# Loading the last v of an attention and spectral-mixing kernel on another queue, in two parts

## Chip, cores and metric

The kernel runs on one core of one Trainium2 chip. The metric is device time in microseconds (us) of one execution; lower is better. Inputs lie in the chip's memory (HBM) when the clock starts, and the output has to be there when it stops.

## What is computed

Two steps follow each other. The first is linear attention over 8 batches x 8 heads with 576 tokens of 64 features; the second mixes the tokens of each batch in the frequency domain, with one complex 512x512 matrix for each of 64 modes, and adds a gated product.

```python
def phi(x):
    proj = np.einsum('bhsd,df->bhsf', x, w_phi)                 # 64 -> 128 features
    proj = proj - np.max(np.abs(proj), axis=-1, keepdims=True)
    return np.concatenate([np.exp(proj), np.exp(-proj)], axis=-1)
q_p, k_p = phi(q), phi(k)
kv  = np.einsum('bhsf,bhsd->bhfd', k_p, v)
num = np.einsum('bhsf,bhfd->bhsd', q_p, kv)
den = np.einsum('bhsf,bhf->bhs', q_p, k_p.sum(2))[..., None] + 1e-06
x   = (num / den) as [8, 576, 512]

X = np.fft.rfft(x, axis=1)                                       # 64 modes are mixed
Yr = Xr @ w_r[m] - Xi @ w_i[m];  Yi = Xr @ w_i[m] + Xi @ w_r[m]
u = x + np.fft.irfft(Y, n=576, axis=1)
out = u + np.maximum(u @ w_ch, 0)
```

The matrices `w_r` and `w_i` are 64 x 512 x 512 in float32 each, and all of them have to be read once. They are the bulk of the 163.64 MB that the kernel reads.

## The kernel before

**Units.** Attention is cut into 16 units: 4 groups `g` of two heads by 4 pairs `bp` of batches. Each unit loads k and q (as bfloat16, converted on the way) and v (`vn`, float32, 128 partitions x 2 batches x 576 elements, 576 KB). Partition p of the load holds nine tokens in a row of one head. In memory that is one run of 2304 bytes for each of the two batches.

**Order.** A hand-written loop over `n` staggers the units: in one turn, unit n+1 has its rows of k and q projected, unit n is finished and unit n-1 goes into the frequency domain. `InOrder` keeps every engine's instructions in the order in which the program writes them. So an engine that waits holds up all that stands behind it.

**v in that loop.** `weigh_v` gets the weights of unit n, `ee`, on ScalarE. `weigh_v2` first copies `ee` into a column of `va` and then multiplies v by it in two VectorE instructions (`va<-vn,ee`), whose result TensorE needs in `kv`. Right after unit n's `weigh_v2`, the loop issues the load of v of unit n+2. The tile `vn` has two buffers, so this load takes the buffer that has just been read. Units 0 and 1 get their v on SyncE's queue (SP) at the start; units 2 to 15 get it on GpSimd's queue (POOL).

**Weights.** The mixing matrices come in 64 loads of 128 partitions x 4 modes x 2 rows x 512 (`wload`), read as float32 and written as bfloat16, in the order of the list `wq`. They are issued on POOL by `next_w`, between the loads of q, k and v, into nine rotating buffers `wt` and a few tiles that are not yet in use. `mix` uses one load: eight matmuls of 512 columns. Mixes are interleaved with attention (`some`), and when attention is over a second loop does the last 20 of them:

```python
    while mixq:
        key = mixq.pop(0)
        ...
        mix(*key, wts.pop(key), XTb[g % 2], bank)
        next_w(1)
        ...
            fill(n)
```

`fill` does the work that lies beside these mixes: products of the channels with `w_ch`, the tables of the inverse transform, and the sums that use finished modes. Its first call comes after the first `mix` of that loop. The finished modes are moved between partitions by small transfers on SP (`yall<-yst`, `zall<-zst`). The last stage sums the rest and stores the output on SP.

**Queues.** Loads with a change of type go through POOL; in the profile its DMA queue is q0 (software_dynamic). SP's is q1 (hardware_dynamic). Between the two loads at the start and the first `yall` store SP issues nothing. q8 carries TensorE's instructions.

**Line numbers.** Since `InOrder` issues each instruction, the profile gives line 37 (L37) for almost all of them. Instructions are told apart by tile: `vn`, `va`, `wt`, `XT` (the modes of x), `xs` (attention's output), `yall` and `zall`.

Of the kernel before, what the change touches and what calls it, by code (L numbers as in the profile page):

```python
# [10 lines left out]
F32 = mybir.dt.float32  # L11
# [6 lines left out]
B_, H_, S_, D_ = 8, 8, 576, 64  # L18
# [25 lines left out]
def kernel(  # L44
# [15 lines left out]
    pool, sp = InOrder(tc, nc.gpsimd), InOrder(tc, nc.sync)  # L60
# [25 lines left out]
    pin = pin_cm.__enter__()  # L86
# [7 lines left out]
    def load(t, src, g, bp, eng):  # L94
        eng.dma_start(
            t.rearrange("p b c d -> p b (c d)"),
            src[2 * bp:2 * bp + 2, 2 * g:2 * g + 2].rearrange("b h (p c) d -> (h p) b (c d)", c=9),
        )


    class Unit:
# [11 lines left out]
        def load_v(self, eng=pool):  # L113
            self.vn = pin.tile([128, 2, 9, D_], F32, name="vn")
            load(self.vn, v, self.g, self.bp, eng)

        def turn(self, src, dst, flat, part):

            rows = src.rearrange("p i c d -> p (i c d)")
            lo, hi = ((0, 4), (4, 9))[part]  # L120
            ptr = one([128, hi - lo, 128], BF16)
            for j in range(lo, hi):
                if flat or j < 4:
                    pe.transpose(ptr[:, j - lo, :], rows[:, j * 128:(j + 1) * 128], ident_b)
                elif j < 8:
                    n = 9 + 2 * (j - 4)
                    pe.transpose(ptr[:, j - lo, :], rows[:, n * 64:n * 64 + 128], ident_b)
                else:
                    for i in range(2):
                        pe.transpose(ptr[64 * i:64 * i + 64, j - lo, :], src[:, i, 8, :], ident_b)  # L130
            act.copy(dst[:, lo:hi, :], ptr)
# [227 lines left out]
    def next_w(n):  # L359
        for _ in range(n):  # L360
            if wq:
                key = wq.pop(0)
                wts[key] = wload(*key)
# [3 lines left out]
    units = [Unit(g, bp) for g in range(NG) for bp in range(NP)]  # L367
# [73 lines left out]
    def forward_table():  # L441

        for p0, p1, d, n in ((0, 128, 0, 4), (0, 64, 4, 1), (64, 128, 5, 1)):
            src = csf[p0:p1, min(d, 4):min(d, 4) + n]
            dst = CF[p0:p1, d:d + n]
            for x in range(2):
                dve.tensor_scalar_mul(
                    out=dst[:, :, :, x, :], scalar1=1.0 - 2.0 * x,
                    in0=src[:, :, x, :].rearrange("p c (t m) -> p c t m", t=2))
        dve.tensor_scalar(out=mi[:, 0:1], in0=pi, scalar1=0, scalar2=1,  # L450
                          op0=ALU.logical_shift_right, op1=ALU.bitwise_and)
        dve.tensor_copy(mf[:, 0:1], mi[:, 0:1])
        for i in range(2):
            for n in range(4):
                sign, b = ((-1.0, 1.0), (1.0, 0.0))[n % 2]
                dve.tensor_scalar(out=side[:, i, n:n + 1], in0=mf[:, 0:1],
                                  scalar1=sign * (1.0 - 2.0 * i), scalar2=b * (1.0 - 2.0 * i),
                                  op0=ALU.mult, op1=ALU.add)
# [29 lines left out]
    def some(n):  # L488
        for _ in range(n):
            if mixq:  # L490
                key = mixq.pop(0)
                mix(*key, wts.pop(key), XTb[key[0] % 2], lambda: one([128, DMODEL]))
                if key not in held:
                    next_w(1)
# [5 lines left out]
    def unit(i):  # L500
        return units[i] if 0 <= i < len(units) else None

    for n in range(-2, len(units) + 1):
        P, Q, K, R = (unit(n + i) for i in (-1, 0, 1, 2))
        X = 0 if n < 4 else 6 if n == 4 else 3
        if Q:
            Q.exp_q(0)
        if K:
            K.rows_k(0)
            K.exp_k(0)  # L510
        if Q:
            Q.weigh_v2()
            if unit(n + 2):
                unit(n + 2).load_v()
        if P:
            P.freq()
            assert not any(key[0] == P.g - 2 for key in mixq)
            P.keep_x()
            if P.bp == NP - 1:
                mixq += [key for key in order if key[0] == P.g and (P.g < 2 or key[1] < 12)]  # L520
        if Q:
            Q.cols_q(1)
            Q.exp_q(1)
        some(1 if X else 0)
        if K:
            K.rows_k(1)
            K.exp_k(1)
        if Q:
            Q.kv()
        some(2 if n == 4 else 0)  # L530
        if K:
            K.rows_q(0)
            K.rows_k(2)
            K.rows_q(2)
            K.rows_q(1)
        if Q:
            Q.cols_q(2)
            Q.keep_kv()
            Q.exp_q(2)
        if K:  # L540
            K.exp_k(2)
            K.weigh_v()
        some(1 if X else 0)
        if R:
            R.turn_k(0)
        if K:
            K.shift_q()
        if R:
            R.turn_k(1)
        if Q:  # L550
            Q.num(0)
        if K:
            K.cols_q(0)
        if R and unit(n + 4):
            unit(n + 4).load_k()
        if Q:
            Q.num(6)
        if R:
            R.turn_q(0)
            R.turn_q(1)  # L560
            if unit(n + 4):
                unit(n + 4).load_q()
        if Q:
            Q.num(12)
        some(X - 2 + (n == 12))
        if n == -1:
            forward_table()
        if n < 3:
            next_w((2, 3, 2, 3, 2)[n + 2])
        elif n == 3:  # L570
            next_w(1)
        if n == 6:
            pool.dma_start(wchb, moe_w_ch.rearrange("(dc p) e -> p dc e", p=128))
# [349 lines left out]
    while mixq:  # L923
# [13 lines left out]
        if left > 8:  # L937
            n = -(-max(len(todo) - A - 2, 0) // (left - 8))
        elif left == 8:
            n = 2  # L940
        else:
            n = math.ceil(len(todo) / max(left - 0.6, 0.4)) if left else 0
# [111 lines left out]
```

## Time and profile before

| | |
|---|---|
| three timed runs | 440.22, 440.20, 439.05 us (median 440.2) |
| profiled execution, first to last instruction | 438.5 us |
| its time apart from the span | not listed; the median of the timed runs is 1.7 us above the span, the lowest 0.55 us |
| TensorE (matmuls) busy | 332.0 us, 76% |
| VectorE busy | 296.4 us, 68% |
| ScalarE busy | 279.4 us, 64% |
| GpSimd busy | 113.0 us, 26% |
| read from HBM | 163.64 MB, 395 GB/s over the span with the writes |
| mean granted TensorE clock | 0.906 |

How to read what follows. Times on the left of a row are microseconds from the first instruction. A row of the timeline gives start, duration, engine, operation, what it writes and reads, how many were merged, and in brackets the idle time of that engine before it with what ended it. A row of the waits gives total, number of times and longest. A DMA has landed when its completion has been counted sixteen times, once for each of the 16 DMA engines that work for a core; the trace holds these sixteen steps with their times. The chain is followed back from the last instruction, at each step to what released it.

### The profile page before, as it was taken

The page shows a single profiled execution, that of the slowest core. Times are in us where ns is not written, and L with a number is a line of the kernel's source. Part 1 is how long each engine was busy: PE and PEld are TensorE (multiplying, and loading weights), DVE is VectorE, ACT ScalarE, POOL GpSimd, SP SyncE. Part 2 cuts the span into 40 slices and gives each one's busy share as a digit, 9 for nine tenths or more (in the row PEclk, how much of TensorE's full clock was granted, in tenths as well). Part 3 has the DMA queues.
Part 4 walks back from the last instruction along what each step waited for, and adds up shares of the span by engine and source line. Part 5 has one row for each costly group of instructions (what it writes and reads, how often), then busy time and mean ns, then how long its engine had stood idle before and what let it go on. Part 6 is the DMA issues. An engine that isn't in the chain of part 4 may idle for free.

```text
span 438.5 us, 10107 instructions
## 1 busy us (share of the span) xinstructions
PE 332.0 (76%) x4190; PEld 202.1 (46%) x4233; DVE 296.4 (68%) x583; ACT 279.4 (64%) x478; POOL 113.0 (26%) x151
## 2 busy tenths in 40 slices
PE   2687678688687687687787787284789999998993
PEld 1355456465465465455465555152444554333320
DVE  5667776765786877976986888243784333886684
ACT  3786786776986886875875876210553442665781
POOL 6232132113221222221222221121101111483072
PEclk9998796789998999996996998876899999999996
DMA  9999999999999999999999999999999999996787
GB/s 213 209 212 210 237 212 237 237 212 248 228 211 239 225 228 232 237 215 235 232 217 239 210 239 211 238 213 212 212 215 223 219 222 224 212 219 135 242 361 309
DMA packets 51710, 99.55 MB, mean 227 GB/s; under 512 B 2512, under 2 KB 13648, under 8 KB 51664
## 3 DMA queue, kind: packets, MB, share of 16 engines
q0 software_dynamic: 45232, 85.86, 99.7%
q1 hardware_dynamic: 6272, 12.98, 8.5%
q8 instruction: 33, 0.54, 0.5%
q14 instruction: 13, 0.11, 0.1%
q10 hardware_dynamic: 160, 0.07, 0.1%
HBM read 163.64 MB, written 9.44 MB: 395 GB/s over the span
## 4 chain that ended last, share of the span: by engine, by line
PE 43%; DVE 22%; ACT 18%; DMA 10%; issue 5%; POOL 0%; POOLq 0%; ACTq 0%; DVEq 0%
PE pt L37 17%; PE one L37 14%; DMA wt<-in_moe_w_r_dram 8%; PE two L37 8%; ACT AB L37 7%; DVE m L37 6%; DVE mk L37 6%; PE pp L37 4%; ACT AQ L37 3%; ACT XT L37 3%; DVE xs L37 2%; DVE XT L37 2%; DMA qb<-in_q_dram 2%; ACT qT L37 1%; DVE yacc L37 1%
## 5 line engine op out<-in xcount | busy, mean ns | idle before, releaser
L37 ACT ACTIVATE AB<-two 128x1024 bf16<-128x1024 f32 x64 | 62.0, 1024 | 10.6 <-DVE mk L37 7.2
L37 ACT ACTIVATE AQ<-two 128x1024 bf16<-128x1024 f32 x64 | 62.6, 1043 | 2.0 <-PE two L37 1.8
L37 ACT CAST xw<-pt 128x512 bf16<-128x512 f32 x50 | 29.4, 588 | 41.9 <-PE pt L37 41.8
L37 DVE TENSOR_REDUCE m<-two 128x8 f32<-128x1024 f32 x32 | 39.2, 1224 | 15.8 <-PE two L37 15.7
L37 DVE TENSOR_TENSOR va<-vn,ee 128x1152 bf16<-128x1152 f32 x32 | 42.0, 1355 | 8.2 <-DMA vn<-in_v_dram 8.2
L37 DVE TENSOR_REDUCE mk<-two 128x8 f32<-128x1024 f32 x32 | 38.9, 1218 | 7.7 <-PE two L37 7.7
L37 POOL DMA_DIRECT2D wt<-in_moe_w_i_dram x28 | 21.0, 750 | 86.4 <-PE pt L37 37.7
L37 POOL DMA_DIRECT2D wt<-in_moe_w_r_dram x30 | 22.5, 751 | 69.2 <-PE one L37 30.7
L37 PE MATMUL pt<-wchb,xT 128*128 128x512 bf16 x127 | 35.6, 393 | 5.2 <-DVE xT L37 3.5
L37 PEld LDWEIGHTS <-xs 128*128 128x128 bf16 x624 | 31.6, 103 | 12.6 <-issue 7.3
L37 PE MATMUL two<-w2blk,qT 128*128 128x256 bf16 x128 | 22.1, 301 | 20.2 <-ACT AB L37 8.4
L37 ACT COPY qT<-one 128x512 bf16<-128x512 bf16 (+1 forms) x32 | 19.3, 641 | 27.5 <-PE one L37 27.2
L37 PEld LDWEIGHTS <-qT 128*128 128x128 bf16 x144 | 14.6, 103 | 36.8 <-issue 33.2
L37 PE MATMUL one<-wt,XT 128*32 128x512 bf16 x304 | 27.5, 452 | 4.9 <-DMA wt<-in_moe_w_i_dram 3.3
L37 PE MATMUL two<-mT,minus 96*128 96x512 bf16 x64 | 28.5, 446 | 3.2 <-issue 1.5
L37 PEld LDWEIGHTS <-AQ 128*128 128x128 bf16 x512 | 25.8, 111 | 8.8 <-issue 5.6
L37 PE MATMUL one<-kvz,AQ 128*128 128x65 bf16 x512 | 28.4, 212 | 1.2 <-ACT qT L37 0.8
L37 DVE COPY xT<-pt 128x512 bf16<-128x512 bf16 x36 | 17.0, 472 | 17.8 <-PE pt L37 17.8
L37 PE MATMUL one<-va,AB 64*128 64x65 bf16 x1024 | 22.5, 199 | 8.3 <-DVE va L37 8.3
L37 DVE RECIPROCAL rd<-one 128x6 f32<-128x6 f32 x48 | 9.4, 196 | 27.6 <-PE one L37 27.5
L37 DVE TENSOR_TENSOR xs<-one,rd 128x384 bf16<-128x384 f32 x48 | 26.7, 557 | 1.6
L37 POOL DMA_DIRECT2D kb<-in_k_dram x16 | 11.4, 714 | 62.2 <-PE one L37 57.2
(151 smaller groups left out, 719.3 us busy)
## 6 DMA issues: line engine op xcount, KB each, us to landing
wt<-in_moe_w_r_dram POOLq DMA_DIRECT2D x30, 1024.0 KB, 28.1
wt<-in_moe_w_i_dram POOLq DMA_DIRECT2D x28, 1024.0 KB, 28.4
out_dram<-of SPq DMA_DIRECT2D x16, 512.0 KB, 4.0
vn<-in_v_dram POOLq DMA_DIRECT2D x14, 576.0 KB, 24.6
kb<-in_k_dram POOLq DMA_DIRECT2D x16, 288.0 KB, 20.4
qb<-in_q_dram POOLq DMA_DIRECT2D x16, 288.0 KB, 18.3
xs<-in_moe_w_i_dram POOLq DMA_DIRECT2D x2, 1024.0 KB, 23.1
vn<-in_v_dram SPq DMA_DIRECT2D x2, 576.0 KB, 4.6
```

What stands on the lines that cost most here:

```text
L37: ins = f(*args, **kwargs)
```

## The change

In the turn of `n = 13`, where the v of the last unit (15) is loaded, the load is no longer issued on POOL as one transfer of 128 partitions. It is issued on SP as two transfers, one of partitions 0 to 101 and one of partitions 102 to 127, into the same tile. All other loads stay as they are. POOL has one issue less, and SP has two more, the only ones between the start and the `yall` stores. On all engines the order of the other instructions is the same.

```diff
+        def load_v_parts(self):
+            self.vn = pin.tile([128, 2, 9, D_], F32, name="vn")
+            dst = self.vn.rearrange("p b c d -> p b (c d)")
+            src = v[2 * self.bp:2 * self.bp + 2, 2 * self.g:2 * self.g + 2].rearrange(
+                "b h (p c) d -> (h p) b (c d)", c=9)
+            for p0, p1 in ((0, 102), (102, 128)):
+                sp.dma_start(dst[p0:p1], src[p0:p1])
...
         if Q:
             Q.weigh_v2()
-            if unit(n + 2):
+            if n + 3 == len(units):
+                unit(n + 2).load_v_parts()
+            elif unit(n + 2):
                 unit(n + 2).load_v()
```

The load that the diff replaces, `load`, is the same with all 128 partitions in one `dma_start` on the engine that it is given.

## The prediction

> **What bounds the kernel now.** I read the page first: its queue rows (packets, MB, share of 16 engines' span) say that one queue, the one POOL feeds, keeps the 16 DMA engines occupied for the whole span.
>
> ```profile
> q0 software_dynamic: 45232, 85.86, 99.7%
> q1 hardware_dynamic: 6272, 12.98, 8.5%
> q8 instruction: 33, 0.54, 0.5%
> ```
>
> The weights `wt` are nearly all of that. Near the end they land one every 4.9 to 6 us, whatever the engines do. The reader should see that q0 has no gap to fill.
>
> Then the waits (engine, line, waited for: us in total, times, longest), for those in which a transfer is late:
>
> ```profile
> DVE va L37 <- DMA vn<-in_v_dram: 8.2, 1, 8.2
> PE one L37 <- DVE va L37: 8.3, 2, 7.7
> PE pt L37 <- DMA wt<-in_moe_w_r_dram: 4.3, 1, 4.3
> PE one L37 <- DMA wt<-in_moe_w_i_dram: 3.3, 1, 3.3
> ```
>
> The first is exactly the transfer that is changed: VectorE stands still 8.2 us for the last unit's v, and TensorE behind it. But two waits of TensorE for weights, 3.3 and 4.3 us, stand close by. Their order in time decides, so next the timeline of TensorE and, last, the chain (start, us, what):
>
> ```profile
> 283.75 0.67 PE L37 MATMUL one<-va,AB 64*128 64x65 bf16 x18 [7.71 <-DVE va L37]
> ...
> 297.11 0.66 PE L37 MATMUL one<-wt,XT 128*32 128x512 bf16 x8 [3.30 <-DMA wt<-in_moe_w_i_dram]
> 302.11 1.08 PE L37 MATMUL pt<-wt,XT 128*32 128x512 bf16 x8 [4.34 <-DMA wt<-in_moe_w_r_dram]
> ```
>
> ```profile
> 265.36 36.71 DMA wt<-in_moe_w_r_dram
> 302.11 1.64 PE pt L37 x11
> ```
>
> The stall for v ends at 283.75. TensorE then does what is left of attention and at 297 and 302 is waiting for weights again. The chain that sets the end does not go through v at all: it runs through the weight issued at 265.36 and landed at 265.36 + 36.71 = 302.07, and from there over TensorE, VectorE and ScalarE to the last store. That weight feeds the first `mix` of the last loop; everything after it in program order (`fill`, tables, stores) cannot pass it. I call it the anchor.
>
> **The change, part by part.**
>
> *The 8.2 us stall.* SP has issued nothing since 1.3 us, so its two transfers wait only for the buffer, which unit 13's weighting leaves at 246.9 (the two `va` multiplies that start at 244.25, 2.62 us). The first load of v on SP landed within 4.0 us. Here the queue is shared: if every packet waits for one of q0 (173 ns), even 38 packets on one engine take 38 x (0.09 + 0.173) = 10 us; with 2 us of start that is 259. VectorE wants v at 274.1 (its copy into `va` starts at 273.89 and takes 0.24). So the stall goes, with 15 us to spare. What is late next: the weights. The last unit's remaining matmuls (283.75 to 292.7, 9 us) would end near 284.5, and the next mixes need weights landing at 287.2, 292.1, 297.1 and 302.1. All 8.2 us turn into longer waits of TensorE before the anchor. Gain on the path: 0. If those weights were early instead, it would be 8.2.
>
> *POOL.* One issue goes (0.71 us), and the waiting for `va` with it. POOL has eight transfers in flight at most: the v issue at 252.66 and the next three come about 0.5 us after the landing of the eighth before them (252.10, 253.59, 258.53, 259.97). Without v the following weights move up one place in that row, 1.5 to 5 us earlier at issue. As q0 is never empty (25 to 37 us from issue to landing) an earlier issue does not land earlier: 0. The two SP issues (some 0.45 us each) have nothing queued behind them until the first `yall` store at 320.40: 0.
>
> *What remains is how much work each DMA engine has to do before the anchor.* v's bytes are the same, and both before and after they lie ahead of the anchor. On q0 v takes 1.49 us (the weight before it lands at 280.82, v at 282.31): 8 rows per engine at 0.184 us. On SP's queue a row is two packets of 2304 bytes; in the packet records of the first loads they follow each other every 90 ns on an engine, so 0.18 us a row. Removed from every engine: 8 x 0.184 = 1.47 us. Added: 0.18 us times the rows that this engine carries. A load has landed when the slowest engine has landed its share, so the question is the slowest engine alone.
>
> The trace tells much of that engine. The anchor's sixteen completion steps come in two groups: eight engines are done 5.4 to 3.7 us before the last, eight within 2.0 us of it (seven of these at 2.0 to 0.6). And TensorE's instruction packets (33 on q8, 16384 bytes) have durations that repeat with a period of eight: 974, 974, 961, 893, 893, 949, 945, 936 ns. Eight engines take turns; the landings slip by about 1.1 us right after packets 1, 9, 17 and 25 (32.6, 117.5, 192.7 and 272.6 us). So the late half fetches instructions, and the engine that is first in turn is last everywhere.
>
> Which rows does that engine get of 102 and 26? Every transfer on SP in this trace has 128, 64 or 16 partitions, in equal shares on 16 engines. 102 and 26 do not divide by 16, so there are three cases, for the engine that ends last:
> - it is left out, or holds only 2 rows of the small part (26 = 13 x 2): -1.47 or -1.47 + 0.36 = -1.11 us;
> - shares as even as can be, 6 or 7 rows and 1 or 2: 7 to 9 rows, -0.2 to +0.15 us;
> - equal shares (102 = 6 x 17) and it is one of the six: 17 + 2 rows, -1.47 + 3.42 = +1.95 us.
>
> The early half can carry 19 rows: +1.95 leaves it 1.7 us or more ahead at the anchor, and its latest member is still 0.56 us ahead at the last weight (2.51 there). I take -1.11, since equal shares are all that the trace shows, six engines of sixteen are a minority, and one row speaks for the last engine being outside them: at 421.3, while it fetches the 33rd instruction packet, the other fifteen begin a store in an otherwise idle queue, and compared with the store before, a starter of the second half of the order is missing, not one of the first.
>
> The Trainium skill ("DMA: Bandwidth & Descriptors", section on why a DMA increments its semaphore by 16) states the same divisor rule, with the lowest-numbered engines taking the work: 6 engines for 102 partitions and 13 for 26; by it the sum is -1.11 or -1.47, or +1.95 if the late engine is among the first six. No run here shows it yet.
>
> The same page's rules for kernel authors speak against the change: two transfers to disjoint partitions share the same 16 engines, so use one of 128; by that the sum is 0. The equal steps of 128-partition loads agree with it, but no row has a split of this kind.
>
> *From the anchor to the end.* Every later mix starts after its weight has landed, by 1.75 us at least until the last one, 0.89 us there (403.11 against 402.22). These weights move with the same engine, so the whole tail shifts with the anchor: 1 to 1. One thing may not shift evenly, the clock: granted 0.50 in the window 302 to 306, 0.70 in 306 to 310, 0.66 in 315 to 320, changing on a fixed raster of 3.41 us. The raster does not move with the work, so the first 18 us of the tail can gain or lose part of a step: half of 3.41 x 0.5 either way, about 0.9 us.
>
> *Sum.* Span 438.5 - 1.1 = 437.4 us. The runs have a median of 440.2, 1.7 us over the profiled span (lowest 439.05). I set the prediction against the median: 440.2 - 1.1 = 439.1 us.
>
> **The rivals.** *Slower: the late engine is one of the six.* Then it has 19 rows in place of 8, and the anchor and all weights behind it land 1.95 us later, from the moment v is on the queue. Place: the landing of the weight that starts the last loop, 304 in place of 302. It decides as soon as the added rows of a late engine exceed 8. With one of the other late engines (0.6 to 2.0 us ahead) it is 0 to 1.35. Time 440.2 + 1.95 = 442.2. For: that one engine's number isn't in the trace. Against: the missing starter.
>
> *Nothing changes: the shares are even.* -0.2 to +0.15: 440.2. For: all rows seen are even. Against: 102 cannot be, in whole equal shares.
>
> *The stall's 8.2 us partly reach the end.* Only the slack of the tail could be won beyond the anchor, at most 0.9 us (the last mix): 440.2 - 1.1 - 0.9 = 438.2. Against: TensorE's order is fixed, and nothing after the anchor can go before it.
>
> **How the numbers follow.** A measurement of this kernel can tell about 0.3% (1.3 us) from no change. Late engine spared: 0.58, in which the left-out case (-1.47) or a lucky clock step takes it past 1.3 us faster (0.31), else it stays within (0.27). Late engine among the six: 0.23, slower. Even shares: 0.12, within 0.10, slower 0.02. Stall's gain reaching the end: 0.07, faster 0.06, within 0.01. Faster 0.37, within 0.38, slower 0.25. Range: below, -1.47 with 0.9 of the clock is 437.8; above, 442.2 of the slower case. The likeliest case alone: 437.8 to 440.0.
>
> **What would show it.** Right: no wait of `va` for v; SP's loads issued at about 247 and landed before 262; TensorE waiting 8 us more in sum before the mixes from 287 to 302; the anchor landing at 301.0, its slowest completion step moved by 1.1 us towards the others while six of the early ones move 1.9 later. Wrong: the anchor at 303 to 304 (the six hold the late engine), unmoved (even shares), or the anchor earlier and the end not (clock or VectorE in the tail). The whole is wrong if the chain after passes through something ahead of the anchor other than that weight.

## The result, and the profile after

The changed kernel takes 441.04 us in the median (440.88 to 441.69, five runs), the kernel before 440.2 (439.05 to 440.22, five runs). The ratio of the runs is 1.0037, with a 95% interval of 1.0026 to 1.0048: slower by 1.1 to 2.1 us. (The two medians alone differ by 0.8 us, 0.19%; the ratio on record is taken over all five runs of each.) The profiled executions have spans of 439.3 and 438.5 us. The forecast was 439.1.

The page's queue rows of the changed kernel (packets, MB, share of 16 engines' span): 0.59 MB have moved from q0 to q1, and q0 is nearly as full as before.

```profile
span 439.3 us, 10157 instructions
...
q0 software_dynamic: 45088, 85.27, 99.2%
q1 hardware_dynamic: 6547, 13.57, 8.9%
q8 instruction: 33, 0.54, 0.4%
```

SP's timeline of the changed kernel has the two issues (start, us, what). Their landings are at 255.8 and 256.0.

```profile
243.09 0.74 SPq L37 DMA_DIRECT2D vn<-in_v_dram  x2
```

The waits for transfers in the changed kernel (us in total, times, longest):

```profile
PE one L37 <- DMA kb<-in_k_dram: 6.6, 1, 6.6
PE one L37 <- DMA wt<-in_moe_w_i_dram: 6.6, 2, 3.8
...
PE one L37 <- DMA wt<-in_moe_w_r_dram: 4.8, 2, 4.3
...
PE pt L37 <- DMA wt<-in_moe_w_r_dram: 4.5, 2, 3.9
...
PE pt L37 <- DMA wt<-in_moe_w_i_dram: 1.1, 2, 0.8
...
DVE va L37 <- DMA vn<-in_v_dram: 0.5, 1, 0.5
```

VectorE's 8.2 us for v are gone. In their place TensorE waits for weights, as its timeline shows (start, us, what, idle time before and what ended it):

```profile
283.03 0.66 PE L37 MATMUL one<-wt,XT 128*32 128x512 bf16 x8 [0.49 <-DMA wt<-in_moe_w_r_dram]
...
287.98 0.66 PE L37 MATMUL one<-wt,XT 128*32 128x512 bf16 x8 [2.78 <-DMA wt<-in_moe_w_i_dram]
292.95 1.08 PE L37 MATMUL one<-wt,XT 128*32 128x512 bf16 x8 [4.31 <-DMA wt<-in_moe_w_r_dram]
297.88 1.08 PE L37 MATMUL one<-wt,XT 128*32 128x512 bf16 x8 [3.85 <-DMA wt<-in_moe_w_i_dram]
302.83 1.08 PE L37 MATMUL pt<-wt,XT 128*32 128x512 bf16 x8 [3.87 <-DMA wt<-in_moe_w_r_dram]
...
404.23 0.66 PE L37 MATMUL pt<-wt,XT 128*32 128x512 bf16 x8 [0.77 <-DMA wt<-in_moe_w_i_dram]
```

0.49 + 2.78 + 4.31 + 3.85 + 3.87 are 15.3 us, where before had 7.6: the stall has become 7.7 us of other waits. The last line is new beside this profile of before, where the same mix did not wait; its weight had landed at 402.22:

```profile
403.11 0.66 PE L37 MATMUL pt<-wt,XT 128*32 128x512 bf16 x8
```

So the chain of waits now runs through that last weight and the transfers before it, and not through the one that I called the anchor (start, us, what):

```profile
283.51 39.09 DMA wt<-in_moe_w_r_dram
...
336.46 31.29 DMA wt<-in_moe_w_r_dram
...
368.76 35.43 DMA wt<-in_moe_w_i_dram
...
404.23 0.69 PE pt L37 x8
```

368.76 + 35.43 is 404.19, 2.0 us later than before. The anchor landed at 302.79 (before 302.07).

Why the weights are later can be read from the anchor's sixteen completion steps, one for each DMA engine. Here they are as distances in us from the first step, whose time stands in front:

```
before  296.67 | 0.0 0.1 0.1 0.2 0.3 1.1 1.1 1.8 3.4 3.4 3.6 3.7 3.9 4.6 4.8 5.4
after   295.73 | 0.0 0.3 0.6 3.5 3.5 3.6 3.6 3.7 3.8 4.1 4.4 4.4 4.5 5.5 5.5 7.1
```

Before, eight engines are early (0 to 1.8) and eight late (3.4 to 5.4). After, three are early, twelve stand together and one is alone at the end. v's own semaphores tell how many engines had rows. That of the first transfer (102 partitions) has one step at its start (243.54) and then six single ones, from 254.1 to 255.8, where a load on all engines has sixteen. That of the second (26) has one at its start and thirteen single ones: seven at 248.6 to 250.0, and six at 255.1 to 256.0, when the first transfer was landing too. I read this as 102 rows on 6 engines, 17 each, and 26 rows on 13 engines, 2 each, the six among the thirteen: six engines have 19 rows, seven have 2, three have none. Before, each had 8. The trace does not name the engine of a step. Shares on 6 and 13 engines are what the divisor rule of the Trainium skill gives ("DMA: Bandwidth & Descriptors", the section on why a DMA increments its semaphore by 16), and this trace agrees with it, 6 and 13.

### The profile page after: what moved, and what is told of

The parts are those of the page before. It is cut to its first block, busy times and chain, and to the rows that moved or that the text cites. A ratio compares the mean times of both kernels' runs of the same rounds, so it can differ in the third digit from the quotient of the medians.

```text
span 439.3 us, 10157 instructions
## 1 busy us (share of the span) xinstructions
PE 327.7 (75%) x4233; PEld 197.9 (45%) x4233; DVE 296.0 (67%) x583; ACT 279.1 (64%) x478; POOL 111.9 (25%) x150
## 4 chain that ended last, share of the span: by engine, by line
DMA 45%; PE 22%; ACT 12%; DVE 12%; issue 8%; POOL 1%; POOLq 0%; ACTq 0%; DVEq 0%
DMA wt<-in_moe_w_r_dram 23%; DMA wt<-in_moe_w_i_dram 15%; PE one L37 11%; DMA vn<-in_v_dram 7%; PE two L37 6%; ACT AB L37 6%; DVE m L37 4%; DVE mk L37 3%; PE pt L37 3%; ACT AQ L37 3%; PE pp L37 2%; ACT XT L37 1%; ACT qT L37 1%; DVE xs L37 1%; DVE XT L37 1%
## 5 line engine op out<-in xcount | busy, mean ns | idle before, releaser
L37 PE MATMUL two<-w2blk,qT 128*128 128x256 bf16 x128 | 20.5, 285 | 20.5 <-ACT AB L37 8.8
L37 PEld LDWEIGHTS <-XT 128*32 128x32 bf16 x512 | 15.0, 150 | 37.5 <-issue 25.0
L37 PEld LDWEIGHTS <-qT 128*128 128x128 bf16 x144 | 14.2, 100 | 36.7 <-issue 33.5
L37 PE MATMUL two<-qT,w2blk 128*128 128x512 bf16 x64 | 27.9, 435 | 3.4 <-ACT AQ L37 3.2
L37 PE MATMUL one<-ident_b,kb 128*128 128x128 bf16 x144 | 17.7, 273 | 15.2 <-DVE ident_b L37 8.2
L37 PEld LDWEIGHTS <-AQ 128*128 128x128 bf16 x512 | 24.8, 109 | 7.9 <-issue 4.5
L37 PE MATMUL one<-kvz,AQ 128*128 128x65 bf16 x512 | 27.4, 209 | 0.9 <-ACT qT L37 0.8
```

The source lines that it names most:

```text
L37: ins = f(*args, **kwargs)
```

## Experiments

The theories: **S**, uneven shares give 19 rows (partitions of v) to a late engine. **Q**, any v on SP's queue costs, beside a full q0. **P**, each transfer, or an odd number of partitions, has a price of its own. **C**, without the stall TensorE's clock is lower and the tail pays. All kernels but the repeats differ from the changed one only in how `load_v_parts` issues v.

**One transfer on SP** (e1), the queue without the split:

```
-            for p0, p1 in ((0, 102), (102, 128)):
+            for p0, p1 in ((0, 128),):
```

> v of the last unit on SP's queue as one transfer of 128 partitions (the split taken out of the change). Theory S (uneven shares: of the six engines that carry 102 partitions one is late anyway, and it gets 19 rows in place of 8): with 128 partitions every engine gets 8 rows again, so the weight that starts the last loop lands within 0.4 us of 302.1, and the time is that of before: ratio 0.999 to 1.001. Theory Q (any v on SP's queue beside a full q0 costs more, split or not): that weight at 302.8 and ratio 1.003 to 1.005, as with the change. Theory C (the stall of VectorE that goes leaves TensorE idle earlier and colder, and the tail pays): the stall goes here too, so ratio 1.003 as well, with the weight at 302.1.

Ratio 1.000 (0.9987 to 1.0013). Here v lands at 252.9 and VectorE's stall for it is gone too, so neither the queue nor the lost stall explains the slower time: against Q and C. The anchor landed at 302.94, where Q had it and not S; the repeat below has 302.33 with the same code, so a single landing does not decide between them. The steps are two groups of eight again, 5.2 us wide.

```
e1      297.75 | 0.0 0.1 0.2 0.3 0.3 0.5 1.1 1.3 2.9 3.3 3.4 3.4 3.6 4.8 5.1 5.2
```

**Two transfers with even shares** (e2):

```
+            for p0, p1 in ((0, 96), (96, 128)):
```

> v of the last unit on SP's queue as two transfers of 96 and 32 partitions, both divisible by 16. Theory S: 6 + 2 = 8 rows on every engine, ratio 0.999 to 1.001 as with one transfer. Theory P (two transfers by themselves, or rows that an engine writes outside of its usual partitions, are what costs): ratio 1.003 or more, as with the change. Theory Q: 1.003 to 1.005.

Ratio 1.000 (0.9985 to 1.0014). The same queue and the same number of transfers as in the changed kernel, whose interval (1.0026 to 1.0048) does not overlap: only the numbers of partitions differ. This pair is what the verdict on S rests on; two transfers as such cost nothing that can be told. TensorE waits here as in the changed kernel, for the anchor and for the last weight:

```profile
302.02 1.08 PE L37 MATMUL pt<-wt,XT 128*32 128x512 bf16 x8 [3.85 <-DMA wt<-in_moe_w_r_dram]
...
403.54 0.66 PE L37 MATMUL pt<-wt,XT 128*32 128x512 bf16 x8 [1.07 <-DMA wt<-in_moe_w_i_dram]
```

So a wait of the last mix does not by itself mean a slower kernel; what counts is when that weight lands.

```
e2      297.11 | 0.0 0.2 0.3 0.5 0.6 0.8 1.6 1.7 3.4 4.1 4.4 4.5 4.6 4.7 4.7 4.9
```

**Shares on five engines** (e3):

```
+            for p0, p1 in ((0, 125), (125, 128)):
```

> v of the last unit on SP's queue as transfers of 125 and 3 partitions: by equal shares 25 rows on five engines and 1 more on three of them, no row on the other eleven. Theory S with the sixth engine as the late one: the engine that is last with the change gets nothing now, and the eight that fetch TensorE's instructions lose 1.47 us each; the five carry 26 rows, +4.2 us at 0.22 us a row, against a lead of 5.4 to 3.6 us. The weight that starts the last loop lands at 301.5 to 302.7, earlier than with the change (302.8), though the five carry more: ratio 0.999 to 1.002. If the late engine is among the first five: the weight at 305 to 306, ratio 1.006 to 1.010. Theories Q and P: slower than the change, since more rows are uneven, 1.004 or more.

Ratio 1.0022 (1.0005 to 1.0039), with the anchor at 303.05: above what S said with the sixth engine late, and below the other forecasts. v's semaphores have 5 and 3 single increments: 25 rows on each of five engines, one more on three of them. The steps are 7.1 us wide, with three early and one alone at the end, as in the changed kernel.

```
e3      295.94 | 0.0 0.3 0.4 3.0 3.8 3.8 3.8 4.0 4.4 4.7 4.8 4.8 5.0 5.6 5.8 7.1
```

Leaving one engine out did not bring the time of before, and it is not clear of the changed kernel either, since the intervals overlap. The last may now be an overloaded early engine: the latest of the early ones stood 1.8 us behind the first step before, and 25 rows at 0.19 us (the price that the kernel with the doubled part shows below) add 4.8, together 6.6. Which engine it is isn't shown.

**The split on POOL's queue** (e4):

```
+            for p0, p1 in ((0, 102), (102, 128)):
+                pool.dma_start(dst[p0:p1], src[p0:p1])
```

> v of the last unit stays on POOL's queue, as two transfers of 102 and 26 partitions (the split alone, without the other queue). Theory S, if POOL's queue shares 102 partitions over all 16 engines (7 rows at most, and 2 of the 26): 9 rows in place of 8, +0.2 us, ratio 0.9995 to 1.001, and VectorE waits for v some 8 us as before. If POOL's queue takes six engines too: the weight at 302.8 or later and ratio 1.002 to 1.005. Theory Q: ratio 1.000, as SP is not used. Theory P: 1.003.

Ratio 1.0081 (1.0059 to 1.0102): a miss upwards for all theories. TensorE's timeline has the anchor at 305.4 and the last weight at 406.9:

```profile
305.43 1.08 PE L37 MATMUL pt<-wt,XT 128*32 128x512 bf16 x8 [3.87 <-DMA wt<-in_moe_w_r_dram]
...
406.98 0.66 PE L37 MATMUL pt<-wt,XT 128*32 128x512 bf16 x8 [0.89 <-DMA wt<-in_moe_w_i_dram]
```

VectorE's wait for v is still there (12.9 us), but TensorE waits for the anchor after it, so the weights set the time. The steps have the shape of uneven shares, 9.0 us wide. Here all sixteen engines raise v's semaphores, but 176 packets of 8 bytes are in this queue that before does not have. 176 is 10 x 17 + 3 x 2, as many as one for each row's place on the engines without data, if the shares are those of SP's queue; that fits, though the trace does not say which engine a packet ran on. In POOL's queue a row is one packet of 4608 bytes; its mean duration is 180 ns in the kernel before and 334 ns here, so that 19 rows cost more than the 3.4 us that I took.

```
e4      296.39 | 0.0 0.4 0.7 4.2 4.3 4.3 4.5 4.9 5.3 5.3 5.4 5.5 6.7 6.7 7.2 9.0
```

**Even shares on POOL's queue** (f4), which tells whether e4 paid for its shares or for a second transfer:

```
+            for p0, p1 in ((0, 96), (96, 128)):
+                pool.dma_start(dst[p0:p1], src[p0:p1])
```

> v stays on POOL's queue, as two transfers of 96 and 32 partitions, both in even shares over 16 engines (102 and 26 on that queue gave 1.0081). Theory S: shares are even, so the time is that of the kernel before, plus at most the second issue on POOL (0.7 us, hidden as weights are in flight for 25 us and more): ratio 0.999 to 1.002, anchor 301.8 to 302.6, steps as before the change, 6.4 us between the weights on both sides of v. If it is the second transfer on POOL's queue that costs (its place among the eight in flight, its issue): 1.004 to 1.008, and 8 us or more between those weights.

Ratio 1.0014 (0.9999 to 1.0029), 5.5 us wide, two groups of eight. v's packets took 266 ns in the mean, and the anchor (303.51) is 0.9 us above what S said, so the second transfer does something here; but most of e4's cost goes with the shares.

**The large part twice** (f1), the suspected cost doubled:

```
+            for p0, p1 in ((0, 102), (0, 102), (102, 128)):
```

> The transfer of 102 partitions goes twice into the same buffer, then that of 26: the suspected cost is doubled. Theory S (shares are equal on as many engines as divide the rows, 6 for 102, and one of the six is a late engine): 17 more rows on each of the six. By the 2.9 us that e4's 19 rows put between two weights (9.30 us between landings, one weight 4.95, one v in even shares 1.47) a row costs 0.23 us, so the last weight lands 17 x 0.23 = 3.9 us after that of the changed kernel (404.2), at 408.1, its last completion step is alone by 4 to 6 us where the changed kernel had 1.1 to 1.5, the three earliest stand 11 to 13 us ahead, and the time is 1.012 to 1.015 of the kernel before. Theory Q (any row on SyncE's queue costs the same, whoever gets it): 102 rows are 6.4 per engine, 1.3 to 1.5 us, ratio 1.006 to 1.008, steps as in the changed kernel. Theory C (a colder TensorE without the stall is the cost): 1.0037 as before.

Ratio 1.0089 (1.0076 to 1.0102), between what S and Q said. The steps decide:

```
f1      295.98 | 0.0 0.6 1.3 3.6 3.7 3.9 4.2 4.3 4.5 4.9 6.6 7.3 7.7 7.7 8.5 9.8
```

The first step stands where it stood in the changed kernel (295.73), so the added rows cost the engines without them nothing: not Q. The groups have come apart, in sizes that uneven shares can give: three early engines and seven late ones outside the six (2 rows or none), five early ones with 36 rows, and one late one with 36 at the end. I had expected that one to be alone by 4 to 6 us, and it is alone by 1.3: I had forgotten that the five beside it get 17 more rows as well. The row's price is in the same line: the five (mean 7.6) against the three (mean 0.6) make 7.0 / 36 = 0.19 us a row, if the three have none. My 0.23 was too dear: 17 x 0.19 = 3.2, and against the changed kernel the anchor came 3.0 us later (305.82 after 302.79), 0.18 a row, and the last weight 2.9. TensorE's timeline:

```profile
305.86 1.08 PE L37 MATMUL pt<-wt,XT 128*32 128x512 bf16 x8 [3.83 <-DMA wt<-in_moe_w_r_dram]
...
407.08 0.66 PE L37 MATMUL pt<-wt,XT 128*32 128x512 bf16 x8 [0.46 <-DMA wt<-in_moe_w_i_dram]
```

**Sixteen transfers of eight partitions** (f2):

```
+            for p0 in range(0, 128, 8):
+                sp.dma_start(dst[p0:p0 + 8], src[p0:p0 + 8])
```

> v on SyncE's queue as 16 transfers of 8 partitions: by theory S 16 rows for each of the first eight engines, none for the other eight. If the eight late (instruction-fetching) engines are the sixth to the thirteenth in the numbering, three of them are loaded: three engines stand at the end of the anchor's completion steps, within 1 to 2 us of each other, and three (the last three in number, without rows and without fetches) are early by 7 us or more; the last weight lands at 403.0 to 404.5, ratio 1.001 to 1.005. If the late engines were spread over the whole numbering, four of them would be loaded and four early ones would stand in front. If the eight late ones were the upper eight, none is loaded: anchor 301 or earlier, ratio 0.997 to 1.000. Theory P (each transfer has a price of its own): 16 issues of 0.4 us on SyncE, which has nothing else then; with 1 us for each start on its queue v would land at 266 or later, still ahead of the 276 at which VectorE wants it.

Ratio 1.0056 (1.0044 to 1.0068) with the last weight at 405.8, both above what S said. Each transfer's semaphore has eight single increments, so eight engines have 16 rows. Two engines stand at the end and two in front, where I expected three and three:

```
f2      298.64 | 0.0 0.1 2.3 2.3 2.3 2.3 2.6 2.6 2.7 2.9 3.1 3.5 3.7 3.7 6.7 6.7
```

More than one loaded late engine, as S needs; but that the order of the engines puts the late ones sixth to thirteenth is not borne out by a count of two. Counted with the other shapes, and if every transfer takes the first engines of one order, it would fit five early engines first in the order (e3 and f3, with five loaded, leave three early ones in front), a late one sixth (the change and f1, six loaded, leave three too), and one early and one late as seventh and eighth; no record names an engine. The first step is 1.6 to 2.0 us later than before (296.67 and 297.08): this is not a matter of shares, and the next kernel is for it.

**Eight transfers of sixteen partitions** (g1): even shares, many transfers.

```
+            for p0 in range(0, 128, 16):
+                sp.dma_start(dst[p0:p0 + 16], src[p0:p0 + 16])
```

> v on SyncE's queue as 8 transfers of 16 partitions: every transfer has one row for each of the 16 engines, so the shares are even, but there are many transfers. Theory S: time as with v in one transfer, ratio 0.999 to 1.002, completion steps of the anchor in two groups of eight, 5.2 to 5.4 us wide. Theory P (a price for each transfer, which the kernel with 16 transfers of 8 partitions would have paid too: 1.0056, 2.5 us): half of that, 1.003, with steps of the same two groups, only all later.

Ratio 1.0038 (1.0023 to 1.0053). Two groups of eight, 5.4 us wide, all of it later:

```
g1      298.19 | 0.0 0.0 0.4 0.5 0.5 1.0 1.4 1.4 3.9 4.0 4.0 4.6 4.6 5.1 5.4 5.4
```

```profile
303.63 1.09 PE L37 MATMUL pt<-wt,XT 128*32 128x512 bf16 x8 [3.88 <-DMA wt<-in_moe_w_r_dram]
...
404.34 0.66 PE L37 MATMUL pt<-wt,XT 128*32 128x512 bf16 x8 [0.97 <-DMA wt<-in_moe_w_i_dram]
```

So P is true as well, for many transfers: 0.38% of 440 us over seven added ones is 0.24 us each. That is no fixed price: fifteen added ones at 0.24 would be 3.6 us, and f2 lost 2.5 in all, with uneven shares besides. For the second transfer of the changed kernel e2 is the measurement: 0.00%, within 0.15% (0.7 us). The two causes look different: here the transfers move the first step and leave the width, uneven shares widen. Why many transfers cost isn't shown.

**Rows for the early engines** (f3), meant to beat both kernels: 19 rows on five engines, 3 on all others.

```
+            for p0, p1 in ((0, 48), (48, 73), (73, 98), (98, 123), (123, 128)):
```

> v on SyncE's queue as transfers of 48, 25, 25, 25 and 5 partitions: by theory S 3 + 15 + 1 = 19 rows for each of the first five engines and 3 for each of the other eleven, so that the sixth engine, the late one that the changed kernel loaded, has 3. The late engines lose 8 rows on POOL's queue (1.47 us) and get 3 at 0.2: 0.8 us earlier than before. The five loaded ones have the margin of the early half, 3.65 us and more at the anchor and 2.5 at the last weight, plus 1.47, for 19 x 0.21 = 4.0 us. So under S the anchor lands at 301.0 to 301.8, the last weight at 401.4 to 402.8, no single engine is late by over 0.8 us, and the ratio is 0.997 to 1.000. If S is right but the late engine is one of the first five: 404 again, 1.003 to 1.004. Theory P (number of transfers, uneven partitions): five of them, four uneven: 1.004 or more. Theory Q: as with v in one transfer, 1.000, and the last weight at 403.3 as there.

Ratio 1.0034 (1.002 to 1.0049): a miss. Again one engine is alone at the end, by 1.1 us at the anchor and by 2.3 at the last weight:

```
f3      296.63 | 0.0 0.6 1.5 3.3 3.3 3.5 3.7 3.7 4.2 4.4 4.4 4.4 4.5 4.7 4.7 5.8
```

The late engines are lighter, but the margin of the early half was less than I had reckoned. At the last weight its latest member stands at 2.9 (before), only 2.5 us ahead of the last; 16 more rows than the others at 0.19 are 3.0. I had also counted the 1.47 us taken from q0 into the margin, though the late engines have it too. That explains 0.5 of the 2.3 us by which the last one is alone; the rest stays open. Four more transfers than in e1 may add to the time, up to 1 us at the price of g1. So no kernel here beats the one before.

**The repeats** (before, changed, one transfer), each profiled once more:

> The kernel before, profiled once more, for how far landings move between executions of one kernel. If the shift of the anchor and of the last weight is the change's: anchor within 0.4 us of 302.07, last weight within 0.6 of 402.22, completion steps in two groups of eight over 5.2 to 5.5 us. If landings scatter by 1 us between executions, differences of the single profiles under 1 us (one transfer on SyncE: last weight at 403.30) say nothing.

> The changed kernel, profiled once more. Theory S: whichever engine fetches first, three engines 2.5 us and more ahead of the others and one alone at the end, 7 us wide at the anchor and 8 to 8.5 at the last weight, which lands at 403.8 to 404.8. If the width came from the order of the instruction fetches in that one execution: 5 to 6 us wide, two groups of eight.

> v in one transfer of 128 partitions on SyncE's queue, profiled once more. If v on that queue in even shares costs 1 us at the weights, as the first profile of it had it (anchor 302.94, last weight 403.30): the same within 0.4. If that was scatter: anchor 301.9 to 302.4, last weight 402.0 to 402.8. Two groups of eight over 5.2 to 5.5 us in both cases.

The second profile of before has the anchor at 302.19 and the last weight at 403.25; its last mix waited for the weight as well. The second of the changed kernel: 303.53 and 405.03. The last weights of these two are later than expected, by 0.4 and 0.2 us. The second with one transfer: 302.33 and 403.48. Landings of one kernel scatter by up to 1 us (before's last weight: 402.22 and 403.25), the shapes do not:

```
before again  297.08 | 0.0 0.2 0.3 0.5 1.1 1.1 1.4 1.5 3.3 3.9 3.9 3.9 4.6 4.8 5.0 5.1
after again   296.26 | 0.0 0.1 0.7 3.0 3.2 3.5 3.7 3.7 3.9 4.3 4.4 4.6 4.7 5.8 5.8 7.3
whole again   297.06 | 0.0 0.1 0.7 1.1 1.1 1.5 1.5 2.2 3.6 3.9 4.0 4.0 4.8 4.8 4.8 5.3
```

TensorE's timeline in that second profile of the changed kernel:

```profile
303.57 1.08 PE L37 MATMUL pt<-wt,XT 128*32 128x512 bf16 x8 [3.87 <-DMA wt<-in_moe_w_r_dram]
...
405.07 0.67 PE L37 MATMUL pt<-wt,XT 128*32 128x512 bf16 x8 [0.46 <-DMA wt<-in_moe_w_i_dram]
```

All kernels together (width: last step less first step, us):

| kernel | rows of v per engine | ratio (95%) | width at the anchor | last weight |
|---|---|---|---|---|
| before (two profiles) | 8, on q0 | 1 | 5.4, 5.1 | 402.2, 403.3 |
| one transfer on SP (two) | 8 | 1.000 (0.9987-1.0013) | 5.2, 5.3 | 403.3, 403.5 |
| 96 + 32 on SP | 8 | 1.000 (0.9985-1.0014) | 4.9 | 403.5 |
| 8 x 16 on SP | 8 | 1.0038 (1.0023-1.0053) | 5.4 | 404.3 |
| 96 + 32 on POOL | 8 | 1.0014 (0.9999-1.0029) | 5.5 | 404.1 |
| 102 + 26 on SP, the change (two) | 19 x6, 2 x7, 0 x3 | 1.0037 (1.0026-1.0048) | 7.1, 7.3 | 404.2, 405.0 |
| 125 + 3 on SP | 26 x3, 25 x2, 0 x11 | 1.0022 (1.0005-1.0039) | 7.1 | 404.3 |
| 48, 3 x 25, 5 on SP | 19 x5, 3 x11 | 1.0034 (1.002-1.0049) | 5.8 | 404.7 |
| 16 x 8 on SP | 16 x8, 0 x8 | 1.0056 (1.0044-1.0068) | 6.7 | 405.8 |
| 102 + 26 on POOL | 19 x6, 2 x7, 0 x3 | 1.0081 (1.0059-1.0102) | 9.0 | 406.9 |
| 102 twice + 26 on SP | 36 x6, 2 x7, 0 x3 | 1.0089 (1.0076-1.0102) | 9.8 | 407.0 |

## Why the prediction was wrong, step by step

**The stall: right.** It went, with 15 us and more to spare, and all of it turned into waits for weights; e1 and e2 lose it too and win nothing. v was issued 4 us earlier than I said (243 instead of 247) and landed at 256, inside the bound of 259, but only for that reason: from issue to landing it took 12.9 us, where I had allowed 12. The first packet of v ran 3.4 us after the issue (246.5 after 243.09), not 2; in the first load of the kernel it is 1.1 us (1.84 after 0.74). One thing I had not named: k of the last unit shares the engines with v now and lands at 255.5 instead of 252.1, and TensorE waits 6.6 us for it. That is hidden in the same way, by weights that are late anyway.

**POOL: its 0 is right, its reason only in part.** The four weights behind v's old place were not issued 1.5 to 5 us earlier: the first went from 254.12 to 256.07, the others from 259.06 to 257.38, from 260.50 to 262.33 and from 265.36 to 265.06. Each was in flight for 32 us or more, before and after, so I see no effect of that on the landings.

**The row's price and the shares: right.** A row costs 0.18 to 0.19 us against my 0.18, and equal shares on 6 and 13 engines was one of my three cases.

**"Which rows does that engine get of 102 and 26?": the step that failed.** I looked for one engine, the last before the change, found evidence that it is outside the six, and took -1.11 us. Whether that engine is outside isn't settled by any run, but the question itself was wrong. A load lands with the slowest of sixteen engines, and after the change another engine can be slowest. Eight engines stood within 2.0 us of the end, and by my own sum 19 rows move any of them by 1.95 us. What counts is whether at least one of these eight is among the six. If six of sixteen were drawn by chance, none of the eight would be among them in 28 of 8008 draws (six out of the other eight, over six out of sixteen), 0.3%. I gave 0.58 to the gain; with the right question a gain was all but excluded, and what was left was a loss of 0 to 1.95 us.

The runs showed this in its place: after the change one engine is alone at the end, 1.5 us behind the next at the anchor in both profiles, and the anchor is later by 1.0 us, not earlier by 1.1. With even shares in the same two transfers (e2) no engine is alone and the ratio is 1.000; with 17 more rows on the six (f1) the last engine is 3.0 us later still.

The sum also forgot the early half at the last weight. By my own figures its latest member, with 19 rows, would stand only 0.56 us ahead of the old last engine there, so no more than 0.56 of the 1.11 us could have come through to that weight.

The rival for this case named the mechanism and the place: "With one of the other late engines (0.6 to 2.0 us ahead) it is 0 to 1.35". The anchor moved by 1.0 us in the mean of two profiles each: the first step is 0.9 earlier (296.88 to 296.00), the width 1.9 more (5.25 to 7.17). I priced the rival at its other end, 1.95, and its time at 442.2; the measured 441.04 lies between that and the time before.

**-1.47 us for an engine without rows: not borne out in full.** The early engines in front moved by 0.9 us at the anchor and 0.8 at the last weight. If some of them hold 2 rows, -1.1 would be due. With even shares on SP, where nothing should move, the first step is 0.2 to 0.9 us later than the mean of before (e1, its repeat, e2), and before's own two profiles differ by 0.4 there. So what is missing of the 1.47 us stays open.

**"1 to 1" from the anchor to the end: wrong.** The last weight moved by 1.9 us where the anchor moved by 1.0: the mean width there went from 5.76 to 8.45. One step of it can be seen: around TensorE's 28th instruction packet (323.5) two weights land 6.59 us apart, and 6.65 in the repeat, where before it is 5.32. I read it so that an engine that is last already gets a fetch there, and that before the same fetch falls to an engine that has time to spare; which engine it is isn't shown. In return the slack of the last mix, 0.89 us in the first profile of before (0.04 in the second), takes up a part. The last mix starts 1.45 us later in the mean (403.20 to 404.65), the span ends 1.3 later (438.53 to 439.82). The chain after the change runs from one transfer to the next, through weights issued ahead of the anchor's landing, which was my own sign that the whole account of the path is wrong: the end is set by the last weight as well as by the anchor.

**The clock: no part in it.** I allowed 0.9 us either way. With the stall gone, e1 and e2 are at 1.000, and from the last mix to the end it is 35.4 and 35.3 us before, 35.0 and 35.3 after. A single execution can stray further: in the profiled one of e2 it is 36.7 us, though the twelve runs of e2 are level with before.

**The skill's rule against two transfers.** By it ("DMA: Bandwidth & Descriptors", rules for kernel authors) the sum was 0, with the advice to use one of 128. The rule speaks of halves, which run on all 16 engines; for two even parts the 0 holds (e2, 1.000). It says nothing of parts that don't divide by 16, and these are what cost here.

## What to carry to other kernels

When the queue is full, a change in how one load is cut must be costed for all engines at once: write down rows per engine, add them to each engine's present place, and take the new maximum, since asking only where the present last engine ends up gave the wrong sign here. In this kernel loads cut into numbers of partitions that divide by 16, and into one or two of them, cost nothing (e1, e2). The spread of a load's completion steps helped to tell what a kernel pays for: shares made it wider (f1), many even transfers made all steps later (g1). And a stall that stands before a later wait was worth nothing while that wait stayed (8.2 us here, e1).

## What was not expected of the hardware

- TensorE's instruction packets mostly last 893 to 975 ns, with a pattern that repeats every eight. Where the pattern begins differs between executions: the first packet took 974 ns in before, 948 in e1, 962 in e2, 935 in e3. If each place in it belongs to one engine, which engine has had one fetch more at a given time is not fixed by the program. It isn't the whole of the scatter: the two profiles of before both begin with 974 and have the last weight 1.0 us apart.
- A packet of v depends on how the load is cut. On POOL's queue 4608 bytes took 180 ns in one transfer, 266 in 96 + 32 and 334 in 102 + 26. On SP's queue 2304 bytes beside a full q0 took 107 ns in one transfer, 110 in 96 + 32, 123 and 117 in 102 + 26 (two profiles), 142 in eight transfers and 157 in sixteen. These are means. The medians are 106 ns in all but the last two (135.5 and 107), and 93 in the two loads at the start of before, most of whose packets ran ahead of q0's first (5.4 us); their mean is 109.
- Cutting a load of 128 rows into eight even transfers on a queue with nothing else to do cost 0.38%, with the completion steps in their old shape.
- On POOL's queue the load in 102 + 26 left 176 packets of 8 bytes, 9 ns each for most, which no other kernel here has in that queue. Their number fits one for each row's place on the engines without data.
